# Window attention and a squared-ReLU feed-forward: the rows g placed 64 bytes further in SBUF

## The chip, the cores and the metric

The kernel runs on one core of a Trainium2 chip. The metric is the device time of one execution in microseconds. The profile of one execution of the kernel before is used throughout: its views show, for each engine, when an instruction started, how long it took and what it waited for. TensorE has two rows in them: PE for matmuls, PEld for the loading of the operand that stays in the array (LDWEIGHTS). The other engines are VectorE (DVE), ScalarE (ACT), GpSimd (POOL) and SyncE (SP), which issues the transfers.

## The reference

Inputs are q, k, v of shape (4, 8, 768, 64), the weights w_in (512 x 2048) and w_out (2048 x 512), and two scalars s and b. Each query attends to the keys within 15 places of it, and beside them to 24 block summaries of its head (maximum of k and mean of v over blocks of 32):

```python
scores_all = concatenate([where(|i - j| < 16, q k^T / 8, -1e9), q k_sum^T / 8 + log(32)])
a = softmax(scores_all)
x = (a @ concatenate([v, v_sum])) as rows of 512, 3072 of them
h = x @ w_in
g = s * relu(h)**2 + b
out = g @ w_out          # 3072 x 512, float32
```

The feed-forward at the end, 3072 x 512 x 2048 multiplications twice, is by far the largest part.

## The kernel before

**Chunks and steps.** The 3072 rows are worked in 12 chunks (`c`) of T = 256 rows. For each chunk, `hidden(c, f)` makes 128 rows of h (transposed: 128 hidden units by 256 tokens) for f = 0 to 15, `activate(c, f)` makes g from them, and `project(c, f)` adds g's product with 128 rows of w_out to two PSUM tiles `po` (128 tokens by 512 each). A plan sorts everything by step: hidden tiles come two at a time, f and f + 1, and the projections follow LAG = 2 steps later, two f at a time as well. So TensorE's order is mostly 24 matmuls of L364 (two hidden tiles), then 12 of L401 (two projections). The attention of the next chunk (scores L266, transposes L314, values L334) is put between them.

**Two parts of each number.** In chunk 0, operands are plain float32 and every matmul is recorded as two passes. From chunk 1 on, each operand is split into a high part and a low part of type float32r (`wh` and `wl`, `xh` and `xl`, `gh` and `gl`), and each product is made of three matmuls: low times high, high times low, high times high. One hidden tile is then 3 x 4 matmuls with 256 passing columns, and one projection is 2 x 3 with 512. In `nc.tensor.matmul(out, a, b)` the first operand, `a`, is the one that is loaded (LDWEIGHTS, 128 columns), and `b` is the one whose columns pass. In `hidden` the weights are loaded and x passes; in `project` g is loaded, and the weights pass:

```python
terms = [(gl, w_h["out", f]), (gh, w_l["out", f]), (gh, w_h["out", f])]
for t in range(T // P):
    for n, (a, w) in enumerate(terms):
        nc.tensor.matmul(po[t], a[:, t * P : (t + 1) * P], w, ...)
```

**How g is made** (`activate`): two ScalarE activations make r (L371, L372), GpSimd makes g (L382), VectorE casts it to `gh` (L384) and makes `gl` = g - gh (L386). `gh` and `gl` have four buffers each. In chunk 0 a single tile `g0` (L374) uses the buffers of `gh`.

**Where things lie.** The tiles of a pool lie one behind another in each partition of SBUF, at multiples of 32 bytes, and the pools follow each other in the order in which they are opened. At the bottom is a scratch area of 16,384 bytes for transfers that GpSimd would describe; this kernel issues all of its transfers from SyncE. Adding up the sizes (four constants, `ident`, `sb_col`, three masks and `mean4` take 2,688 bytes) gives these places in bytes from the start of a partition:

| tile | first address | bytes of one buffer | modulo 256 |
|---|---|---|---|
| `wh` (pool `slots`, both sides of an f, 2,048 bytes each) | 19,072 | 4,096 | 128 |
| `wf`, `wl` (pool `wring`) | 84,608 | 2,048 | 128 |
| `x`, `xh` | 173,888 | 4,096 | 64 |
| `g0`, `gh` (4 buffers) | 184,128 | 1,024 | 64 |
| `xl` | 192,320 | 4,096 | 64 |
| `gl` (4 buffers) | 202,560 | 1,024 | 64 |

The slices that a matmul takes begin at multiples of 512 bytes in these tiles (weights for L364, g for L401) or of 1,024 (x), so every slice has its tile's place modulo 256.

Of the kernel before, what the change touches and what calls it, by code (L numbers as in the profile page):

```python
# [10 lines left out]
F32 = mybir.dt.float32  # L11
F32R = mybir.dt.float32r
# [6 lines left out]
P = 128  # L19
# [9 lines left out]
T = NSUB * SUB  # L29
# [5 lines left out]
NF = DFF // P  # L35
NEG = -8.0e9
LAG = 2


def win_start(st):  # L40
# [4 lines left out]
def windowed_attention_then_relu2_ffn(ctx, tc, qk, vwin, kt, vt, kq, vrow, wp, sb, out):  # L45


    nc = tc.nc
# [5 lines left out]
    p2 = ctx.enter_context(tc.tile_pool(name="p2", bufs=2))  # L54
# [34 lines left out]
    def at(step, order, fn, *args):  # L89
        plan[step].append((order, len(plan[step]), fn, args))  # L90
# [277 lines left out]
    def activate(c, f):  # L368
        ph = ph_of.pop((c, f))
        r = p2.tile([P, T], F32, name="r")  # L370
        nc.scalar.activation(r, ph, AF.Relu)  # L371
        nc.scalar.activation(r, r, AF.Square)  # L372
        if c == 0:
            g = p2.tile([P, T], F32, name="g0", tag="gh", bufs=4)  # L374
            if f < 2:
                nc.vector.tensor_scalar(g, r, s_col, b_col, ALU.mult, ALU.add)
            else:
                nc.scalar.activation(g, r, AF.Identity, bias=b_col, scale=s_col)  # L378
            gg[c, f] = (g,)
            return  # L380
        g = p2.tile([P, T], F32, name="g")
        nc.gpsimd.tensor_scalar(g, r, s_col, b_col, ALU.mult, ALU.add)  # L382
        gh = p2.tile([P, T], F32R, name="gh", tag="gh", bufs=4)
        nc.vector.tensor_copy(gh, g)  # L384
        gl = p2.tile([P, T], F32R, name="gl", bufs=4)
        nc.vector.tensor_tensor(gl, g, gh.bitcast(F32), ALU.subtract)  # L386
        gg[c, f] = gh, gl

# [107 lines left out]
    for i in range(NC * NF):  # L496
        c, f = divmod(i, NF)

        at(i if c == 0 else i - i % 2, HID, hidden, c, f)
        at(i, CHAIN, activate, c, f)  # L500
        at(i + LAG if i + LAG < NF else (i + LAG) | 1, PROJ, project, c, f)
        if f == NF - 1:
            at((i + LAG) | 1, EVICT, evict, c)

# [58 lines left out]
```

## Time and profile before

| | us |
|---|---|
| median of 3 runs | 648.41 (648.28 to 649.06) |
| the profiled execution | 648.77 |
| its span, first to last instruction | 647.1 |
| PE busy | 630.3, 5164 instructions |
| DVE busy | 332.7 |
| ACT busy | 338.4 |
| POOL busy | 153.8 |

The page of the profile gives each engine's busy time and its share of the span; matmuls are pipelined, so their recorded durations overlap, and a matmul's cost in a row of matmuls is the distance from its start to the next one's start. The chain of waits follows the work back from the last instruction to what released it, and so says what the end hung on. The timeline lists instructions by start time, in hundredths of a microsecond; a row with x4 stands for four of a kind in a row.

### The profile page before, as it was taken

To read this page: it belongs to the slowest core of one execution; us is meant where nothing else is said; L and a number is where in the kernel's file an instruction comes from. 1 tells how busy PE (TensorE), PEld (TensorE's weight loads), DVE (VectorE), ACT (ScalarE), POOL (GpSimd) and SP (SyncE) were. 2 spreads that over 40 slices of the span, in tenths; PEclk is the share of its full clock that TensorE was granted. 3 is DMA by queue.
4 is the path that set the end of the run, shared out by engine and by line. 5 is a ranking of instruction groups with operands and counts; after the bars stand their busy time and mean duration, and the time that the engine had idled before them with its cause. 6 is when DMAs were issued, how large, how long until landed. Compare 5 with 4: busy or idle time off the path is not lost.

```text
span 647.1 us, 13906 instructions
## 1 busy us (share of the span) xinstructions
PE 630.3 (97%) x5164; PEld 549.1 (85%) x5164; DVE 332.7 (51%) x1088; ACT 338.4 (52%) x986; POOL 153.8 (24%) x324
## 2 busy tenths in 40 slices
PE   6799999999999999999999999999999999999997
PEld 4566568989989899898999899898998989999996
DVE  5799988885443434356434434447443353342221
ACT  4899998845444435535435345444444444452322
POOL 3000004143133132232231331331322322312221
PEclk9999999999999999999999999999999999999999
DMA  9999405035203204124402301504420320100000
GB/s 323 386 383 355 131 1 187 1 102 191 72 1 104 72 2 139 49 84 141 141 1 63 115 2 34 153 23 132 146 66 2 105 72 2 57 3 1 33 2 33
DMA packets 25604, 63.25 MB, mean 98 GB/s; under 512 B 3968, under 2 KB 3968, under 8 KB 25536
## 3 DMA queue, kind: packets, MB, share of 16 engines
q1 hardware_dynamic: 25536, 62.36, 29.3%
q8 instruction: 41, 0.67, 0.4%
q14 instruction: 27, 0.22, 0.1%
HBM read 55.90 MB, written 6.29 MB: 96 GB/s over the span
## 4 chain that ended last, share of the span: by engine, by line
PE 86%; ACT 7%; DMA 4%; DVE 2%; issue 0%; SPq 0%; DVEq 0%
PE po L401 39%; PE ph L364 38%; PE pav L334 4%; PE ps L266 3%; PE pt L314 3%; DMA wraw<-in_wp_dram 3%; ACT wraw L116 2%; ACT wraw L117 2%; ACT g L378 1%; DMA kq<-in_kq_dram 1%; ACT pr L298 1%; ACT r L372 1%; ACT r L371 0%; DVE wf_out L134 0%; DVE wf_out L132 0%; DVE wf_in L132 0%
## 5 line engine op out<-in xcount | busy, mean ns | idle before, releaser
L382 POOL TENSOR_SCALAR g<-r,sb_col 128x256 f32<-128x256 f32 x176 | 101.7, 578 | 418.5 <-ACT r L372 322.0
L384 DVE CAST gh<-g 128x256 fp32r<-128x256 f32 x176 | 52.4, 298 | 269.9 <-POOL g L382 269.6
L371 ACT ACTIVATE r<-ph 128x256 f32<-128x256 f32 x192 | 73.4, 382 | 203.8 <-PE ph L364 203.2
L401 PE MATMUL po<-wh,gl 128*128 128x512 f32 x352 | 143.2, 407 | 0.0
L401 PE MATMUL po<-wh,gh 128*128 128x512 f32 x352 | 138.6, 394 | 0.0
L401 PE MATMUL po<-wl_out,gh 128*128 128x512 f32 x352 | 137.7, 391 | 0.0
L364 PE MATMUL ph<-xh,wl_in 128*128 128x256 f32 x704 | 110.9, 280 | 0.0
L364 PE MATMUL ph<-xl,wh 128*128 128x256 f32 x704 | 108.7, 276 | 0.0
L364 PE MATMUL ph<-xh,wh 128*128 128x256 f32 x704 | 108.7, 276 | 0.0
L364 PEld LDWEIGHTS ph<-xh,wl_in 128*128 128x128 f32 x704 | 100.2, 188 | 8.2 <-ACT r L372 0.5
L364 PEld LDWEIGHTS ph<-xl,wh 128*128 128x128 f32 x704 | 93.8, 188 | 0.0
L364 PEld LDWEIGHTS ph<-xh,wh 128*128 128x128 f32 x704 | 92.9, 188 | 0.0
L372 ACT ACTIVATE r<-r 128x256 f32<-128x256 f32 x192 | 80.4, 419 | 6.1
L386 DVE TENSOR_TENSOR gl<-g,gh 128x256 fp32r<-128x256 f32 x176 | 76.4, 434 | 6.0
L401 PEld LDWEIGHTS po<-wh,gh 128*128 128x128 f32 x352 | 66.1, 188 | 14.3
L401 PEld LDWEIGHTS po<-wh,gl 128*128 128x128 f32 x352 | 66.2, 188 | 14.1 <-issue 3.0
L401 PEld LDWEIGHTS po<-wl_out,gh 128*128 128x128 f32 x352 | 66.3, 188 | 11.5
L298 ACT ACTIVATE pr<-pr,mn 128x120 f32<-128x120 f32 x176 | 67.4, 386 | 3.5 <-DVE mn L285 3.3
L321 ACT COPY pT<-pt 120x512 f32<-120x512 f32 x48 | 28.2, 587 | 37.0 <-PE pt L314 36.8
L364 PEld LDWEIGHTS ph<-x,wf_in 128*128 128x128 f32 x128 | 25.0, 200 | 14.3 <-issue 2.6
L244 POOL COPY vw<-vsum 24x256 f32<-24x256 f32 x80 | 36.8, 500 | 1.3
L308 DVE TENSOR_TENSOR pr<-pr,rs 128x480 f32<-128x480 f32 x48 | 35.4, 737 | 1.7
(71 smaller groups left out, 615.6 us busy)
## 6 DMA issues: line engine op xcount, KB each, us to landing
wraw<-in_wp_dram SPq DMA_DIRECT2D x32, 512.0 KB, 10.0
qk<-in_qk_dram SPq DMA_DIRECT2D x44, 368.0 KB, 4.7
vw<-in_vwin_dram SPq DMA_DIRECT2D x48, 192.0 KB, 4.2
out_dram<-o SPq DMA_DIRECT2D x24, 256.0 KB, 2.0
kraw<-in_kt_dram SPq DMA_DIRECT2D x12, 384.0 KB, 3.4
vraw<-in_vt_dram SPq DMA_DIRECT2D x12, 252.0 KB, 4.7
kq<-in_kq_dram SPq DMA_DIRECT2D x4, 512.0 KB, 4.6
vraw<-in_vt_dram SPq DMA_DIRECT2D x6, 264.0 KB, 7.0
```

The costliest lines, as they stand in the source:

```text
L244: filler(c).tensor_copy(vw_t[c, p][WIN:KR, e], vsum[bi][WIN : WIN + NB, 2 * p + e, :].unsqueeze(1).to_broadcast([NB, NSUB, D]),)
L298: nc.scalar.activation(pr, pr, AF.Exp, bias=mn_of[c, p][:, n : n + 1], scale=-1.0, accum_out=sm_of[c, p][:, n : n + 1])
L308: nc.vector.tensor_tensor(pr, pr, rs.unsqueeze(2).to_broadcast([P, 4, KR]), ALU.mult)
L321: nc.scalar.copy(pT_of[c, p], pt_of.pop((c, p))[:KR])
L334: nc.tensor.matmul(o[64 * e : 64 * e + 64, i * SUB : (i + 1) * SUB], vw[:, e, i, :], pT[:, e * T + i * SUB : e * T + (i + 1) * SUB], start ...
L364: nc.tensor.matmul(ph, w[:, kc * P : (kc + 1) * P], x[:, kc], start=(n == 0), stop=(n == len(terms) - 1))
L371: nc.scalar.activation(r, ph, AF.Relu)
L372: nc.scalar.activation(r, r, AF.Square)
L382: nc.gpsimd.tensor_scalar(g, r, s_col, b_col, ALU.mult, ALU.add)
L384: nc.vector.tensor_copy(gh, g)
L386: nc.vector.tensor_tensor(gl, g, gh.bitcast(F32), ALU.subtract)
L401: nc.tensor.matmul(po[t], a[:, t * P : (t + 1) * P], w, start=(f == 0 and n == 0), stop=(f == NF - 1 and n == len(terms) - 1),)
```

## The change

The tiles `gh`, `gl` and `g0` become 512 bytes longer. `gh` and `gl` use 1,024 bytes of their tile from byte 64 on (GAP = 16 elements of 4 bytes), `g0` the first 1,024. The scratch area shrinks to 2,048 bytes, which makes room. `gl` is asked for before the cast instead of after it.

```diff
+GAP = 16
...
         if c == 0:
-            g = p2.tile([P, T], F32, name="g0", tag="gh", bufs=4)
+            g = p2.tile([P, T + 128], F32, name="g0", tag="gh", bufs=4)[:, :T]
...
-        gh = p2.tile([P, T], F32R, name="gh", tag="gh", bufs=4)
+
+        gh, gl = p2.tile([P, T + 128], F32R, name="gh", tag="gh", bufs=4), p2.tile([P, T + 128], F32R, name="gl", bufs=4)
+        gh, gl = gh[:, GAP : GAP + T], gl[:, GAP : GAP + T]
         nc.vector.tensor_copy(gh, g)
-        gl = p2.tile([P, T], F32R, name="gl", bufs=4)
         nc.vector.tensor_tensor(gl, g, gh.bitcast(F32), ALU.subtract)
...
-    nc = _bacc.Bacc("TRN2", target_bir_lowering=False, num_devices=1)
+    nc = _bacc.Bacc("TRN2", target_bir_lowering=False, num_devices=1, dynamic_dma_scratch_size=2048)
```

By the same sums, all tiles move down by 14,336 bytes (56 x 256), those behind `gh` up again by 2,048, and those behind `gl` by 2,048 more. Modulo 256, `gh` and `gl` then lie at 128, and all the others of the table where they were (`g0` at 64). Modulo 512, the passing weights lie at 128 and the slices of `gh` and `gl` at 384.

## The prediction, made before the changed kernel was run

> **What bounds the kernel now.** I read the page first, then the chain of waits in order of time, then the timeline of TensorE alone, because only the last shows how far apart two matmuls start.
>
> ```profile
> span 647.1 us, 13906 instructions
> ...
> PE 630.3 (97%) x5164; PEld 549.1 (85%) x5164; DVE 332.7 (51%) x1088; ACT 338.4 (52%) x986; POOL 153.8 (24%) x324
> ...
> PEclk9999999999999999999999999999999999999999
> ...
> PE 86%; ACT 7%; DMA 4%; DVE 2%; issue 0%; SPq 0%; DVEq 0%
> PE po L401 39%; PE ph L364 38%; PE pav L334 4%; PE ps L266 3%; PE pt L314 3%; DMA wraw<-in_wp_dram 3%; ACT wraw L116 2%; ACT wraw L117 2%; ACT g L378 1%; DMA kq<-in_kq_dram 1%; ACT pr L298 1%; ACT r L372 1%; ACT r L371 0%; DVE wf_out L134 0%; DVE wf_out L132 0%; DVE wf_in L132 0%
> ```
>
> TensorE is the bound: 86% of the chain that ended last, at a full granted clock. The projection matmuls of L401, the ones whose operand the change moves, hold 39% of the span, some 252 us. So the question is what one of them takes.
>
> ```profile
> 92.24 1.72 PE po L401 x4
> ...
> 401.96 2.75 PE ph L364 x24
> 405.15 2.77 PE po L401 x12
> 407.92 2.74 PE ph L364 x24
> ...
> 632.39 2.75 PE po L401 x12
> 635.14 2.75 PE ph L364 x24
> 637.88 5.51 PE po L401 x24
> ```
>
> These are pieces of the chain: start, length, what, how many. Twelve L401 matmuls take 2.75 us, 24 in a row 5.51 us: 0.2292 to 0.2296 us each, with 512 passing columns. The row at 92.24 is chunk 0, plain float32, where every matmul is two passes: 0.430 us for a pass. The float32r matmuls of the later chunks pass twice as many columns per time. Half of 0.430 would be 0.215 us, so a projection matmul takes 0.014 us more than its doubled rate would give. That excess, 1056 x 0.014 = 14.8 us of the span, is all that this change can touch from above.
>
> Nothing else is late. In the view of TensorE's waits, no row at all names L401, and the longest are these, all from before 97 us:
>
> ```profile
> PE ps L269 <- DMA kq<-in_kq_dram: 4.7, 1, 4.7
> PE ph L364 <- DVE wf_in L134: 2.7, 3, 1.9
> ```
>
> **Which reads meet.** The program's addresses (front part) put, modulo 256 bytes, every weight row (`wh`, `wl`) at 128, every `xh`, `xl` slice at 64, and every slice of `gh` and `gl` at 64. In L401 g is what TensorE loads (LDWEIGHTS) and w is what passes; in L364 w is loaded and x passes. The timeline of loads beside that of matmuls:
>
> ```profile
> 407.30 0.19 PEld L401 LDWEIGHTS po<-wh,gh 128*128 128x128 f32 x1
> 407.52 0.19 PEld L364 LDWEIGHTS ph<-xh,wl_in 128*128 128x128 f32 x1
> ```
>
> ```profile
> 407.06 0.39 PE L401 MATMUL po<-wh,gl 128*128 128x512 f32 x1
> 407.30 0.39 PE L401 MATMUL po<-wl_out,gh 128*128 128x512 f32 x1
> 407.52 0.40 PE L401 MATMUL po<-wh,gh 128*128 128x512 f32 x1
> 407.76 0.63 PE L364 MATMUL ph<-xh,wl_in 128*128 128x256 f32 x4
> ```
>
> The load for the next matmul starts in the same hundredth as the matmul now passing (407.30 and 407.52 in both). So the pair that can disturb each other is the passing operand of one matmul and the loaded operand of the **next**, and both begin together. Call "offset" the place of the loaded operand less that of the passing one, modulo 256. Before: 192 for nearly all of L401, 64 for nearly all of L364. After: 0 for L401.
>
> **Offset 0 already occurs in this trace**, and this carries the forecast. After the last L401 matmul of an odd f, `wh` passes (128) while the next hidden tile's `wl_in` is loaded (128). The second pair of rows above is such a place: 407.52 to 407.76, 0.24 us. There are 86 of them in the timeline; the first and the last:
>
> ```profile
> 105.76 0.40 PE L401 MATMUL po<-wh,gh 128*128 128x512 f32 x1
> 106.00 0.63 PE L364 MATMUL ph<-xh,wl_in 128*128 128x256 f32 x4
> ...
> 634.75 0.39 PE L401 MATMUL po<-wh,gh 128*128 128x512 f32 x1
> 634.98 0.64 PE L364 MATMUL ph<-xh,wl_in 128*128 128x256 f32 x4
> ```
>
> 24 of the 86 distances read 0.24 and 62 read 0.23; their mean is 0.2328 us. That is 0.0036 us above the 0.2292 of the neighbours at offset 192. It is far from the 0.215 that an undisturbed matmul would take.
>
> Could it be the change of stage, and not the offset? The other change of stage, L364 to L401, has offset 0 too, with 256 passing columns:
>
> ```profile
> 107.38 0.62 PE L364 MATMUL ph<-xh,wl_in 128*128 128x256 f32 x4
> 107.83 0.62 PE L364 MATMUL ph<-xl,wh 128*128 128x256 f32 x4
> 108.28 0.62 PE L364 MATMUL ph<-xh,wh 128*128 128x256 f32 x4
> 108.74 0.60 PE L314 MATMUL pt<-ident,pr 128*120 128x128 f32 x4
> ...
> 637.27 0.62 PE L364 MATMUL ph<-xh,wh 128*128 128x256 f32 x4
> 637.72 0.39 PE L401 MATMUL po<-wh,gl 128*128 128x512 f32 x1
> ```
>
> Twelve hidden matmuls take 1.36 us, 0.1133 each. The last four before a projection, whose fourth has offset 0, take 0.45, or 0.1125 each: the same within the rounding. A change of stage alone costs nothing there, and offset 0 neither helps nor hurts with 256 columns.
>
> One sentence of the Trainium skill speaks against any effect. TensorE: Matmul & The Clock Gate, "Step-by-step: what each phase is for", says: "Loading the next tile's weights doesn't steal SBUF read bandwidth from the running matmul." By the same page, "Back-to-back issue gap", 512 columns would take about 216 ns (an estimate from its 512 / 2.4 + 2.5); the half-rate row of chunk 0 agrees (0.215), the float32r rows (0.229) do not. By that rule the change does nothing and the time stays 648.4, the second rival below.
>
> **The change part by part.**
> - *g moved by 64 bytes.* No instruction is added or removed. 1056 L401 matmuls; 87 of them keep their neighbour (86 at offset 0 as counted, one at the very end). 969 go from offset 192 to 0. At 0.0036 us each: **+3.5 us**. Bounds from both sides: if every one read 0.24, as 24 of the 86 do, 969 x 0.0108 = +10.5; if the excess vanished, 969 x (0.215 - 0.2292) = -13.8. I take the 86 places, since they have the same 512 passing columns, the same 128x128 load and the very offset. They lie at a multiple of 512, though, and the new ones at an odd multiple of 256, so the case rests on 256 being the period.
> - *L364 to L401.* `gl` is now loaded at offset 64 while `xh` passes, as in all of L364: nothing.
> - *Writing gh and gl 64 bytes further.* The rows are:
>
> ```profile
> L384 DVE CAST gh<-g 128x256 fp32r<-128x256 f32 x176 | 52.4, 298 | 269.9 <-POOL g L382 269.6
> ...
> L386 DVE TENSOR_TENSOR gl<-g,gh 128x256 fp32r<-128x256 f32 x176 | 76.4, 434 | 6.0
> ```
>
>   Same shapes, contiguous as before: nothing. Were a cast as slow as the subtraction, 136 ns x 176 = 24 us would fall on DVE, which is busy 51%, and two steps (LAG) of about 2.75 us lie between g and its use; without that cover a late `gl` would stall L401 by up to 24 us. Above, DVE idled 269.6 us waiting for POOL's g, so the cover is there. Below nothing: no gain, since no row of TensorE waits for them. Asking for `gl` before the cast issues nothing and leaves the order of the queues as it was.
> - *The scratch.* It shrinks from 16,384 to 2,048 bytes, which moves all tiles down by 14,336 = 56 x 256: no place modulo 256 changes. All data moves through one hardware queue, and the only others are instruction fetches:
>
> ```profile
> q1 hardware_dynamic: 25536, 62.36, 29.3%
> q8 instruction: 41, 0.67, 0.4%
> ```
>
>   Nothing uses the scratch in those rows, so nothing; a gain has no place to come from.
> - *g0 of chunk 0* stays at 64, and its passes have no excess: nothing.
>
> Sum: 3.5 us on the span, 647.1 to 650.6. The profiled execution took 648.77 with 1.7 around the span; the median of the runs shown is 648.41, 0.36 less. So 648.4 + 3.5 = **651.9 us**. A measurement of this kernel tells about 0.2%, 1.3 us, from no change.
>
> **The rivals.**
> - *The excess is a meeting of the two reads which the new offset avoids* (faster). At offset 64 with 256 columns, 0.1133 us is 0.2267 for two, less than 0.2292: so an offset other than 192 may do better. Partial: 969 x 0.0025 = -2.4, 646.0; full, the 0.215 of the half-rate row: -13.8, 634.6. For it: the excess exists only where columns pass at full rate. Against: 86 places at offset 0 that show all of it. It decides if these places are special, or if the period is 512 and not 256. Chance 0.38, of which 0.2 to about 2 to 8 us and the rest beyond.
> - *The offset plays no part* (or 86 places differ by their stage alone): 648.4. For it: the 62 places that read 0.23, and 0.1125 against 0.1133 above. Against: the 24 that read 0.24. That the change would not do what it says is excluded by the addresses. Chance 0.20.
> - *Each offset-0 matmul pays the 0.24 of the dearer places*: +10.5 us, 658.9, or some way towards it. It decides if the state of TensorE that gives 0.24 sustains itself. Since the distances are rounded to hundredths, most of this is the forecast's own upper part; 0.05 beyond 656.
>
> **How the numbers follow.** Slower 0.42 (the forecast 0.37, the dearest places 0.05), within 0.2% 0.20, faster by over 0.2% 0.38. The likeliest case has its own range of 650 to 656. The range for 8 in 10 takes that, the unchanged case, and the faster one down to a gain of 7.5 us (0.26 of its 0.38): 641 to 656, with 0.12 left out below and 0.05 above.
>
> **What would show it.** In the chain, pieces of twelve L401 matmuls at 2.79 to 2.80 instead of 2.75, and the last 24 at about 5.60 instead of 5.51; L364 pieces of 24 unchanged at 2.75; the 86 places as now. Pieces of 2.72 would mean the partial rival, 2.58 the full one, 2.75 no effect. DVE rows of 298 and 434 ns and no L401 row among TensorE's waits would confirm the zero terms. The prediction is wrong if the 86 places owe their 0.0036 us to the change of stage, or if a run of equal offsets settles into another rhythm than a single one shows.

## The result, and the profile after

The changed kernel takes 653.59 us (653.18 to 653.77, 4 runs) against 648.49 of the kernel before on the same chip: a ratio of 1.0076, with a 95% interval of 1.0059 to 1.0094. It is slower by 5.1 us where 3.5 was forecast. The time came out nearly as predicted; the way to it did not. In the whole record one run, of the kernel of experiment 4, stands apart at 1611.77 us, for a reason that no trace shows, and its ratio leaves it out. The page of the changed kernel, its span, busy time and chain (L401 is now L403, L364 is L365):

```profile
span 652.0 us, 13906 instructions
...
PE 633.7 (97%) x5164; PEld 554.3 (85%) x5164; DVE 332.8 (51%) x1088; ACT 339.5 (52%) x986; POOL 152.7 (23%) x324
...
PE 86%; ACT 9%; DMA 3%; SPq 1%; issue 0%; DVE 0%
```

Nothing changed in kind: TensorE still holds 86% of the chain. The pieces of that chain, in order of time (start, length, what, how many), show where the 4.9 us of the span came from:

```profile
631.81 2.72 PE po L403 x12
634.53 2.83 PE ph L365 x24
637.36 2.72 PE po L403 x12
640.07 2.83 PE ph L365 x24
642.90 5.45 PE po L403 x24
```

The projection, whose loads moved, became **faster**: 2.72 instead of 2.75 for twelve, 5.45 instead of 5.51 for the last 24. The hidden stage, whose own operands keep their places to each other, became **slower**: 2.83 instead of 2.75 for 24. Summed over the whole trace, from each float32r matmul's start to the next start on TensorE, the projection takes 245.7 us instead of 247.9 (-2.2) and the hidden stage 251.4 instead of 244.2 (+7.2); TensorE's other matmuls, summed in the same way, take 146.3 instead of 146.2.

The places that carried the forecast look different too. The timeline of TensorE at the end of a projection pair:

```profile
410.11 0.39 PE L403 MATMUL po<-wl_out,gh 128*128 128x512 f32 x1
410.34 0.39 PE L403 MATMUL po<-wh,gh 128*128 128x512 f32 x1
410.57 0.63 PE L365 MATMUL ph<-xh,wl_in 128*128 128x256 f32 x4
411.04 0.63 PE L365 MATMUL ph<-xl,wh 128*128 128x256 f32 x4
411.51 0.64 PE L365 MATMUL ph<-xh,wh 128*128 128x256 f32 x4
```

The pair at offset 0 (410.34 to 410.57) was at offset 0 before as well; in nanoseconds of the trace the 86 such distances were 230 to 236 and are now all 226 or 227. So their 0.0036 us belonged to what came before them, not to the offset alone. Before the change, matmuls at offset 192 stood 226, 229 and 232 ns apart in turn. 46 of the 86 places came third in that turn and read 230 or 231, no more than a third one at offset 192; the 40 others came second, where 229 was due, and read 235 or 236. Each group of four hidden matmuls takes 0.47 where it took 0.45. VectorE's two rows are as forecast, 297 and 434 ns:

```profile
L388 DVE TENSOR_TENSOR gl<-g,gh 128x256 fp32r<-128x256 f32 x176 | 76.4, 434 | 6.0
...
L387 DVE CAST gh<-g 128x256 fp32r<-128x256 f32 x176 | 52.3, 297 | 273.9 <-POOL g L383 273.6
```

### The profile page after: what moved, and what is told of

The parts are those of the page before. It is cut to its first block, busy times and chain, and to the rows that moved or that the text cites. A ratio compares the mean times of both kernels' runs of the same rounds, so it can differ in the third digit from the quotient of the medians.

```text
span 652.0 us, 13906 instructions
## 1 busy us (share of the span) xinstructions
PE 633.7 (97%) x5164; PEld 554.3 (85%) x5164; DVE 332.8 (51%) x1088; ACT 339.5 (52%) x986; POOL 152.7 (23%) x324
## 4 chain that ended last, share of the span: by engine, by line
PE 86%; ACT 9%; DMA 3%; SPq 1%; issue 0%; DVE 0%
PE po L403 39%; PE ph L365 38%; PE pav L335 4%; PE ps L267 3%; DMA wraw<-in_wp_dram 3%; PE pt L315 3%; ACT wraw L117 3%; ACT wraw L118 3%; ACT pr L299 1%; ACT g L379 1%; ACT r L373 1%; ACT r L372 1%; SPq L221 0%; ACT pT L322 0%; SPq L191 0%
## 5 line engine op out<-in xcount | busy, mean ns | idle before, releaser
L403 PE MATMUL po<-wh,gl 128*128 128x512 f32 x352 | 142.8, 406 | 0.0
L403 PE MATMUL po<-wl_out,gh 128*128 128x512 f32 x352 | 137.4, 390 | 0.0
L403 PE MATMUL po<-wh,gh 128*128 128x512 f32 x352 | 137.1, 390 | 0.0
L365 PE MATMUL ph<-xh,wl_in 128*128 128x256 f32 x704 | 112.4, 282 | 0.0
L365 PE MATMUL ph<-xh,wh 128*128 128x256 f32 x704 | 111.6, 281 | 0.0
L365 PE MATMUL ph<-xl,wh 128*128 128x256 f32 x704 | 111.6, 281 | 0.0
L365 PEld LDWEIGHTS ph<-xh,wl_in 128*128 128x128 f32 x704 | 101.4, 189 | 7.7 <-issue 0.5
L365 PEld LDWEIGHTS ph<-xh,wh 128*128 128x128 f32 x704 | 95.9, 190 | 0.0
L365 PEld LDWEIGHTS ph<-xl,wh 128*128 128x128 f32 x704 | 95.2, 189 | 0.0
L403 PEld LDWEIGHTS po<-wh,gh 128*128 128x128 f32 x352 | 66.1, 188 | 14.1
L403 PEld LDWEIGHTS po<-wh,gl 128*128 128x128 f32 x352 | 66.1, 188 | 13.9 <-issue 3.0
L403 PEld LDWEIGHTS po<-wl_out,gh 128*128 128x128 f32 x352 | 66.3, 188 | 10.5
L365 PEld LDWEIGHTS ph<-x,wf_in 128*128 128x128 f32 x128 | 23.7, 190 | 15.7 <-ACT r L372 4.1
```

Source lines behind the costliest of these rows:

```text
L365: nc.tensor.matmul(ph, w[:, kc * P : (kc + 1) * P], x[:, kc], start=(n == 0), stop=(n == len(terms) - 1))
L403: nc.tensor.matmul(po[t], a[:, t * P : (t + 1) * P], w, start=(f == 0 and n == 0), stop=(f == NF - 1 and n == len(terms) - 1),)
```

## Experiments

**What has to be told apart.** Why does a stage slow down whose operands were not touched? In nanoseconds of the trace, the distances in a run of equal matmuls repeat. These are six of a run of projection matmuls and the first twelve of a pair of hidden tiles, from the last chunk, where no attention work stands between:

```
before   projection 226 229 232 226 229 231   hidden 117 117 117 123 118 113 114 113 113 114 113 113
after    projection 227 226 227 227 226 227   hidden 118 117 118 118 117 119 117 118 118 118 117 118
```

A run settles in a rhythm. My theory, the **rhythm theory**: the hidden stage has two rhythms at these offsets, 113.3 ns and 117.8 ns apart, and the moment at which it begins, so the way in which the projection ends, decides which one it falls into. Three rivals: the **displacement theory** (its tiles moved by 14,336 and 2,048 bytes), the **writing theory** (VectorE's writes of gh and gl at the new place disturb it), and later the **fixed-place theory** (each offset has its price wherever it stands, and 0 is the cheapest).

Rows of the kernel before that I had passed over speak for the rhythm theory. Its chain of waits around the end of chunk 0:

```profile
93.95 2.74 PE ph L364 x24
96.69 3.43 PE po L401 x8
100.13 2.83 PE ph L364 x24
102.96 0.44 PE pt L314 x4
103.39 2.77 PE po L401 x12
106.16 2.74 PE ph L364 x24
```

A hidden pair is the 24 matmuls of two hidden tiles. Those at 93.95 and 100.13 both follow projections of chunk 0 in plain float32; the first takes 2.74 and the second 2.83, and the next pair, with its operands at the same places modulo 256, 2.74 again. Both rhythms were there before the change. Call a pair slow when its distances settle at 117.8 ns or more and fast when they settle at 113.3: in the whole trace, 1 of 88 pairs was slow before, and 87 of 88 after.

**1. Other places of g** (four kernels; each a change of one or two lines, timed against the kernel before).

```diff
-GAP = 16
+GAP = 0
```

This is gap0; gap32 and gap48 have 32 and 48 elements there, and gh_only moves gh alone.

> The changed kernel with GAP = 0: the same longer tiles and the small scratch, but gh and gl begin at 64 modulo 256 as before. Rhythm theory (the hidden matmuls fell into a slower rhythm, 0.118 instead of 0.1133 us apart, because the projections before them now end differently): all as before, pieces of 12 projection matmuls at 2.75, of 24 hidden ones at 2.75, about 648.5 us. Rival, displacement theory (the hidden stage is slower because its tiles moved by 14,336 and 2,048 bytes): hidden pieces stay at 2.83, projection pieces return to 2.75, about 655 us.

gap0: 648.95 us, ratio 0.9998 (0.9988 to 1.0007). Its chain:

```profile
633.22 2.75 PE po L403 x12
635.97 2.75 PE ph L365 x24
638.72 5.51 PE po L403 x24
```

These are the old lengths in full, with the small scratch and the longer tiles in place. The displacement theory falls; the 64 bytes alone do it.

> GAP = 32: gh and gl begin at 192 modulo 256, offset 64 in the projection, as the hidden matmuls have it. Rhythm theory: hidden pieces are either 2.75 or 2.83 and nothing between, whatever the projection takes. Rival, writing theory (VectorE's writes of gh and gl at a place other than 64 disturb the hidden matmuls): hidden pieces at 2.83 or another value above 2.75. For the projection neither theory has a number; if offset 64 does there what it does in the hidden stage before, 2.72.

gap32: 654.31 us, ratio 1.0078 (1.0061 to 1.0095).

```profile
604.48 2.79 PE po L403 x12
607.27 2.83 PE ph L365 x24
610.11 2.80 PE po L403 x12
612.90 2.74 PE ph L365 x24
```

> GAP = 48: gh and gl begin at 0 modulo 256, offset 128 in the projection. Rhythm theory: hidden pieces 2.75 or 2.83. Writing theory: above 2.75. Projection pieces: unknown, between 2.60 (no excess, 12 x 0.215 and the switch) and 2.85.

gap48: 651.78 us, ratio 1.0041 (1.0026 to 1.0056).

```profile
602.12 2.78 PE po L403 x12
604.89 2.73 PE ph L365 x24
607.62 2.77 PE po L403 x12
610.40 2.83 PE ph L365 x24
```

```diff
-        gh, gl = gh[:, GAP : GAP + T], gl[:, GAP : GAP + T]
+        gh, gl = gh[:, GAP : GAP + T], gl[:, :T]
```

> Only gh lies 64 bytes further, gl at 64 as before: two of three projection loads at offset 0, one at 192. If the offset acts on each matmul by itself, projection pieces lie at two thirds of the way, 2.73. Rhythm theory: hidden pieces 2.75 or 2.83, nothing between. Writing theory: hidden pieces between, about 2.79, since half of the writes are at the new place.

gh_only: 651.66 us, ratio 1.0037 (1.0024 to 1.0051); its last hidden pieces are 2.75 and the projections between them 2.77:

```profile
632.54 2.75 PE ph L365 x24
635.29 2.77 PE po L403 x12
638.07 2.75 PE ph L365 x24
```

The hidden lengths are the telling ones. In the last chunk of gap32 and gap48 they take turns, 2.83 and 2.74 or 2.73, within one kernel, at the same places, with the same writes by VectorE going on. Of 88 pairs, 24 are slow in gap32, 24 in gap48, 20 in gh_only, and none lies between the two rhythms. The writing theory asked for one value in each kernel and falls. What tells the pairs of one kernel apart is how the projection ahead of them ended. The distance from its last matmul to the pair is 229 or 230 ns for the slow pairs of gap32 and 233 to 236 for its fast pairs, 226 or 227 against 229 to 233 in gap48, and 226 or 227 against 231 to 236 in gh_only, without exception among the 86 pairs of each that follow float32r projections. One such distance does not decide for all kernels: 229 goes with slow pairs in gap32 and with fast pairs in gap48. For the projection, offset 64, which I had guessed at 2.72, is the dearest (2.79 to 2.80), and the mixture gh_only is not two thirds of the way (2.73) but dearer than both (2.77). So a matmul's distance is not a price of its own offset that can be added up.

**2. The moment.** If the moment decides, a shift of a nanosecond or two should turn the rhythm, with every operand in place modulo 256. One more matmul, which adds zeros, stands at the end of each odd f but the last of a chunk, and the number of its columns sets when it ends. Its tile of zeros moves the tiles behind it by 512 bytes, alike in all three kernels, and lies at 128 by the same sums as the other tiles, so it too is at offset 0:

```diff
+    zero = const.tile([P, P], F32R, name="zero")
+    nc.scalar.mul(zero, ident, 0.0)
...
+        if c > 0 and f % 2 and f < NF - 1:
+            nc.tensor.matmul(po[1][:, :EXTRA], zero, w_h["out", f][:, :EXTRA], start=False, stop=False)
```

> The changed kernel with one more matmul at the end of each odd f below 15 (80 of them): a tile of zeros is loaded and all 512 columns of the last weights pass into po, which adds nothing. It is work that the kernel doesn't need. Both theories: 80 x 0.227 = 18.2 us more, about 671.8 us; since one more matmul of the steady rhythm comes before the hidden stage, the rhythm theory too leaves the hidden pieces at 2.83.

> The same, but 508 columns of the extra matmul pass: it ends 4 / 512 x 0.215 = 1.7 ns earlier, nothing else differs. Rhythm theory: the moment at which the hidden stage begins decides, so some of these shifts turn it to 2.75 (3 of the 4 other endings measured did): 671.8 - 80 x 0.08 = 665.4; the hidden pieces after f = 15, which have no extra matmul, stay at 2.83. Rival, that the hidden stage's rhythm hangs on what its own operands or VectorE's writes do: 2.83 everywhere, 671.7.

> The same with 504 columns, 3.4 ns earlier than with 512. Rhythm theory: at least one of 508 and 504 has hidden pieces of 2.75 (about 665.4 us), except after f = 15. Rival: 2.83 everywhere, 671.5.

One run of each: 670.84 us with 512 columns, **664.05 with 508**, 670.61 with 504. (There are 77 added matmuls and not 80 as the expectations count them, 7 in each of 11 chunks: 17.5 us, which fits 670.84 better.) Their chains at the same place of the program; L411 is the added matmul. With 512:

```profile
405.17 2.94 PE po L406 x12
408.12 0.23 PE po L411
408.35 2.83 PE ph L368 x24
```

With 508:

```profile
401.71 2.94 PE po L406 x12
404.66 0.23 PE po L411
404.88 2.72 PE ph L368 x24
407.60 2.73 PE po L406 x12
410.34 2.83 PE ph L368 x24
```

With 504:

```profile
405.13 2.94 PE po L406 x12
408.08 0.22 PE po L411
408.30 2.82 PE ph L368 x24
```

This settles it between the theories: what comes ahead of the hidden stage decides its rhythm. Four columns fewer, some 1.7 ns, and the hidden stage behind it takes 2.72 instead of 2.83; four fewer again, and it is back at 2.82. The control is in the same trace: the piece at 410.34 follows f = 15, which has no extra matmul, and is slow. In the trace of extra508, the 76 pairs behind an extra matmul whose distance reads 225 ns are all fast, and the 10 behind an ordinary end of 226 or 227 all slow. The kernel gains 6.8 us from it, 8.0 in the hidden stage's sum (251.4 to 243.4), less small losses elsewhere. The rival had 671.7 and 671.5: about right for 504, wrong by 7.6 for 508. Columns and moment change together here, so these three kernels alone don't tell them apart; but the endings in gap32, gap48 and gh_only differ while 512 columns pass every time, which speaks for the moment. Each kernel ran once; the runs of the kernel before spread over less than 2 us (647.98 to 649.66), and the 76 and 10 pairs are compared within one trace.

**3. Other places of x.** With the projection at its cheap offset 0, can the hidden stage be had fast by moving x?

```diff
+                xh, xl = p2.tile([P, NKC * T + 128], F32R, name="xh", tag="xh"), p2.tile([P, NKC * T + 128], F32R, name="xl")
+                xt[c] = [x[:, XGAP : XGAP + NKC * T].rearrange("p (k t) -> p k t", t=T) for x in (xh, xl)]
```

with XGAP of 16, 32 and 48 elements.

> The changed kernel with xh and xl 64 bytes further too: offset 0 in the hidden stage as in the projection, only one in the whole loop. Rhythm theory: the hidden stage has rhythms of its own for each offset; what helps the projection (0.2267 at offset 0) need not help here, so 2.72 or 2.83 or a new value. Fixed-place theory (offset 0 is best for any pair): hidden pieces at 2.72, projection at 2.72, about 645 us. If it stays at 2.83: 653.6.

> The same with xh and xl 128 bytes further (192 modulo 256): offset 192 in the hidden stage, 0 in the projection. Rhythm theory: projection pieces stay at 2.72 (its pairs are as in the changed kernel); hidden pieces at 2.72, 2.83 or a new value. Fixed-place theory: offset 192, which cost the projection 0.2292 against 0.2267, makes the hidden stage no better than 2.83, at least 653.

> The same with xh and xl 192 bytes further (0 modulo 256): offset 128 in the hidden stage, 0 in the projection. Rhythm theory: projection 2.72, hidden 2.72, 2.83 or a new value; if 2.72, the kernel is faster than before, about 645 us. Fixed-place theory has no number here beyond the 2.77 to 2.78 that offset 128 gave the projection.

All three lost: 659.86 (1.0166, 1.0149 to 1.0183), 656.08 (1.0107, 1.0092 to 1.0123) and 661.61 us (1.0195, 1.018 to 1.021). The chains, with x at 128 (offset 0 everywhere):

```profile
618.10 2.87 PE ph L367 x24
620.97 2.75 PE po L405 x12
```

and at 0 (offset 128 in the hidden stage):

```profile
619.49 2.88 PE ph L367 x24
622.36 2.76 PE po L405 x12
```

With x at 192 the hidden pieces are 2.83 and the projections 2.76. All 88 hidden pairs of each are slow, settled at 117.8 ns with x at 192 and at about 120 in the two others. Offset 0 gives the projection its best rhythm and the hidden stage a bad one, so the fixed-place theory falls: it had 2.72 here. The projection suffered as well, 2.75 to 2.77 although its own offsets stayed. It too needs some matmuls to settle: with x at 128 it begins with 233, 236, 228, 233 and 231 ns before it reaches 226.7. That the moment at which the hidden stage lets it begin makes this start is what the theory says; no run shows it alone. The rhythm theory had not said which value would come in these three, so they only fit it; they don't test it.

**4. A kernel made by the theory.** Keep offset 0 in the projection, but let it end as it ended before: in odd f, the second half of gh, which the last two loads take, lies at 64 again. The tile of gh is now `whole`, and STEP is 176 elements:

```diff
+        gh = whole[:, GAP : GAP + 2 * STEP].rearrange("p (t n) -> p t n", n=STEP)[:, :, :P]
+        g, gl3 = [x.rearrange("p (t n) -> p t n", n=P) for x in (g, gl)]
+        nc.vector.tensor_copy(gh, g)
+        nc.vector.tensor_tensor(gl3, g, gh.bitcast(F32), ALU.subtract)
```

> The changed kernel, but in odd f the second half of gh lies at 64 modulo 256 (element 192 of its tile), so that the last two loads of g before a hidden stage are at offset 192 as before the change, and the other four of that f at 0. Rhythm theory: the projection keeps its 0.2267 up to there and then ends as it ended before the change (226, 229 and 231 ns), so the hidden stage falls into its fast rhythm: projection pieces at about 2.73, hidden ones at 2.75, 88 x (0.02 + 0.00) = 1.8 us less than before, about 646.6 us, faster than both kernels. Rival, that each place acts by itself: hidden pieces stay at 2.83, projection 2.72 to 2.73, about 654 us.

```profile
628.59 2.75 PE ph L366 x24
631.34 2.74 PE po L413 x12
634.08 2.75 PE ph L366 x24
636.82 5.50 PE po L413 x24
```

The last three distances before a hidden stage read 226, 229 and 231 ns, as written down beforehand, within 1 ns at 84 of 86 places, and 87 of 88 hidden pairs are fast. That is the theory's strongest success: moving two loads back turned a stage of 24 others from 2.83 to 2.75. As a faster kernel it failed. It takes 648.75 us, ratio 0.9993 (0.9984 to 1.0002), which is no difference, where 646.6 was expected: the projection now begins behind the fast hidden stage with 232, 232 and 231 ns before it settles at 226.7, so twelve take 2.74 and not 2.73, and the sums of the two stages are 247.2 and 244.5 us against 247.9 and 244.2 before.

## Why the prediction was right, and where it was wrong

- *TensorE bounds, no other engine matters*: right. No row of its waits names the projection after the change either, and the writes of gh and gl kept their durations.
- *Scratch, longer tiles, order of gl: nothing*: right, shown by gap0.
- *969 pairs at +0.0036 us, +3.5 in all*: this is the step that failed, and with it the sign of its term. The projection gained 2.2 us. The 86 places were read as the price of offset 0, but each is a single matmul at offset 0 behind a run at offset 192, and its distance hung on where in the turn of 226, 229 and 232 ns the run ended. One place in a turn was compared with the mean of the turn. The prediction had named this way of being wrong: that "a run of equal offsets settles into another rhythm than a single one shows". It does, at 226.7 ns.
- *L364 pieces of 24 unchanged at 2.75*: wrong, and this is where the time went, 7.2 us. A stage was costed at nothing because its own operands kept their offsets. The prediction looked for a cost of the change of stage only in the last four hidden matmuls before a projection (0.1125 against 0.1133); the first five of the pair printed above, which it didn't look at, read 117, 117, 117, 123 and 118 ns before the rest settled at 113.3. No rival had it either: the slower rival put its cost into the projection. The row at 100.13 could have warned me.
- *The faster rival, partial*, gave the projection its right size: 0.2267 per matmul, -2.4 us, against -2.2 measured. But it had this from offset 64 in the hidden stage, and in the projection offset 64 turned out the dearest (2.79 to 2.80 for twelve in gap32), so the agreement is in part luck. Its total of 646.0 would have needed the hidden stage to stay. The full rival's 0.215 was half of a float32 pass and no more than an estimate: no run of projections in any trace settled below 226.7 ns.
- *The rule cited from the Trainium skill* (TensorE: Matmul & The Clock Gate, "Step-by-step: what each phase is for"), by which the load of the next weights takes no read bandwidth from the running matmul, was taken as a rule under which nothing changes. The runs do not agree with that for float32r: moving only what is loaded changed twelve projections between 2.72 and 2.80. Whether bandwidth is what is lost there, no run shows. The estimate of 216 ns that the prediction took from the same page of the Trainium skill, "Back-to-back issue gap", rests on a formula that the section gives for the gap of a single matmul, not for a row of loads and matmuls as here.

So the time fell into the range, near its likeliest value, by two errors of opposite sign: +3.5 forecast where -2.2 came, and 0 where +7.2 came. That was luck; the mechanism that the prediction named is not the one that made the kernel slower.

What stays open: what in the chip sets the rhythms. The runs show that the offset and the moment of the start both matter, not which memory or clock makes it so. Only steps of 64 bytes were tried, and no run was made to test that the period is 256 bytes. One sign for it is in last_two: its two loads lie 448 bytes from the passing weights modulo 512, where before the change they lay 192 from them, and the same 226, 229 and 231 ns came. All of these places are added up from the sizes of the tiles; no view shows an address.

## What to carry to other kernels

Where one engine runs the same kind of instruction for most of the time, look at the distances between starts over whole runs, stage by stage, and look for two values of the same stage in one trace: they can be a sign that its speed hangs on how it is entered. A placement is then judged by the total and not by the stage that it touches, and a gain of a per cent from an alignment may be a rhythm that the next edit upstream turns off. The price of a single odd pair does not carry over to a run of them.

## What the runs showed of the hardware that was not expected

- The rhythms that can be read off these traces for float32r matmuls have periods that are multiples of about 6.67 ns: 113.3 and 226.7 (17 and 34 times), 120 with x at 128 (18 times), 233.3 in gap32 behind attention work (35 times), and cycles of three such as 226 + 229 + 232 = 687 (103 times) or 117 + 118 + 118 = 353 (53 times).
- The rhythm depends on the place of the loaded operand against the passing one. For 512 passing columns and with x where it was, the projection pieces of twelve between hidden stages read 2.75 at offset 192, 2.72 at 0, 2.79 to 2.80 at 64, and 2.77 to 2.78 at 128.
- A shift of 1.7 ns before a run of 24 matmuls changes its length by 0.11 us, 4%, and 77 such shifts change the kernel's time by 6.8 us, 1%.
- The plain float32 passes of chunk 0 stand 0.429 to 0.430 us apart before and after the change, at offset 192 both times; no other offset was tried for them.
